# Attention followed by a gated squared-ReLU mixture on one core: one scale for each weight matrix, and two vector operands moved to PSUM

## The chip, the cores and the metric

The kernel runs on one core of a Trainium2 chip. The metric is the device time of one execution in microseconds (us); it ran three times before the change, and the profiled execution is a run of its own. The core has five engines that run their own instruction streams in order and wait for each other through semaphores: PE (TensorE, matrix products; PEld are its weight loads), DVE (VectorE), ACT (ScalarE), POOL (GpSimd) and SP (SyncE, which here only issues DMAs). PE writes PSUM, which has eight banks of 512 float32 columns here; DVE and ACT read and write both PSUM and SBUF.

## The reference, cut to what matters

The inputs are `q`, `k`, `v` of 8 batches x 12 heads x 448 tokens x 64, two gains, and the mixture's parameters. The three weight matrices arrive as 64-bit floats.

```python
def rmsnorm(x, g):
    rms = np.sqrt(np.mean(x * x, axis=-1, keepdims=True) + 1e-06)
    return x / rms * g
q_n, k_n = (rmsnorm(q, g_q), rmsnorm(k, g_k))
scores = scale * np.matmul(q_n, k_n.transpose(0, 1, 3, 2))
scores = scores - np.max(scores, axis=-1, keepdims=True)
attn = np.exp(scores)
attn = attn / (np.sum(attn, axis=-1, keepdims=True) + 1e-09)
x = np.matmul(attn, v)                  # then [8, 448, 768]: heads side by side
...
xk = mu_k * x + (1.0 - mu_k) * x_prev   # x_prev: the token before
xr = mu_r * x + (1.0 - mu_r) * x_prev
k = np.maximum(xk @ w_k, 0.0)           # 768 x 1024
v = k * k @ w_v                         # 1024 x 768
r = 1.0 / (1.0 + np.exp(-(xr @ w_r)))   # 768 x 768
return (r * v).astype(np.float32)
```

## The kernel before

**What a unit of work is.** The 96 heads are taken as 24 "quads" of two head pairs. `load` brings a quad's `q` and `k`, `stats` forms the sums of squares and their reciprocal roots (`rsqrt`: a first guess by integer arithmetic and three Newton steps, 13 small DVE instructions with two scalings ahead of them), `preps` scales `q` and `k` by them and turns them round, and `scores` makes seven groups of score tiles from each quad, two PSUM tiles of 448 columns a group: 168 groups, 336 score tiles. From the fourth quad on every float32 operand is split into two 16-bit parts (high and low) and a product is three 16-bit products. `expo` takes a score tile's maximum on DVE and its exponential on ACT, `probs` and `split` scale and split it, and `attends` multiplies a head pair's probabilities by `v` (48 of these; six make a batch).

**The mixture.** For each batch, `mixk` and `mixr` call `mix` six times each: one product with the earlier token on POOL, one multiply-add on DVE, the high part on ACT, the low part on POOL. That makes 96 mixes. `moe` then has two stages for a batch. The **first stage** multiplies by `w_k` (eight blocks of 18 matrix products, weights `wkh`/`wkl`) and squares the result (`square`). The **output stage** multiplies by `w_r` and `w_v` (weights `wrh`, `wrl`, `wvh`, `wvl`) and ends in `gate`, `store` and the output DMA. Because the first batch needs the weights, `moe` waits in the first batch for all of `w_k` before the first stage and for all 20 weight tiles (`st["wdone"] == NW`) before the output stage.

**The weights.** A tile is 128 columns of a matrix; `w_k` has 8 tiles, `w_r` and `w_v` 6 each. `wload` issues two DMAs a tile on ACT's queue, each of 3 or 4 runs of 1 KB a partition. `weights` turns each half tile from 64-bit to 32-bit floats: one byte's worth of low bits on POOL (written back into the raw buffer), the top word on ACT into a PSUM bank, and a shift-and-or of the two on DVE. `wsplit` then finds a power of two for the tile: the sums of squares of its columns as a matrix product with itself on PE, the diagonal on DVE (`dg`), a second product with ones to spread it over the partitions, a maximum and two small integer steps on DVE into `WSC`. With that scale it writes the high part (ACT) and the low part (DVE, or POOL together with the scaling, for tiles 1 to 13).

**What sets the order.** Nothing above runs in the order of the code. Each of these functions is a generator that yields its next instruction; the class `Plan` keeps an estimated clock for each engine and for each buffer, and takes again and again the instruction whose engine and operands are free earliest, less a priority. The priority of the weights (`wprio`) grows with the planned time and falls with each finished tile (`W_GAP`). The result is one fixed order for each engine, which the chip executes as it stands. The eight PSUM banks are one ring, from which "shares" take up to a number of banks: scores 5 (leaving one free), mixture 2, other 2.

Of the kernel before, what the change touches and what calls it, by code (L numbers as in the profile page):

```python
# [1 line left out]

# [29 lines left out]
WF_BUFS = 2  # L32
# [6 lines left out]
LOW_TILES = range(0, 20)  # L39
POOL_TILES = range(1, 14)  # L40
# [48 lines left out]
WB_A = 'ot'  # L89
WB_B = 'mm'  # L90
# [5 lines left out]
W_GAP = 10e3  # L96
# [108 lines left out]

class Plan:
    LAT = 35

    def __init__(self, tc):
        self.tc = tc  # L210
        self.clk = dict.fromkeys(("PE", "DVE", "ACT", "POOL", "SP"), 0.0)
        self.last, self.use, self.threads = {}, {}, []
        self.form, self.dma_free, self.acc, self.n = None, {"SP": 0.0, "ACT": 0.0}, False, 0
        self.held = {"DVE": [], "POOL": []}

# [13 lines left out]
    def spawn(self, gen, prio=0):  # L229
        th = [gen, prio, None, 0.0]  # L230
        self.threads.append(th)
        self.advance(th)
# [14 lines left out]
    def advance(self, th):  # L247
# [7 lines left out]
        th[2] = x  # L255
        th[3] = self.ready(x) if isinstance(x, list) else 0.0
# [68 lines left out]
    def run(self):  # L325
        while self.threads:
            best, key = None, None
            for th in list(self.threads):
# [11 lines left out]
                k = max(self.clk[th[2][0].eng] + wait, th[3] + slack) - PS * (th[1]() if callable(th[1]) else th[1])  # L340
# [100 lines left out]
def attn_moe_kernel(tc, q, k, v, g_q, g_k, mu_k, mu_r, w_k, w_v, w_r, out):  # L441
# [15 lines left out]
    banks = {n: Share(psum, *c) for n, c in (("sc", SC_SHARE), ("mm", MM_SHARE), ("ot", OT_SHARE))}  # L457
# [18 lines left out]
    for nm, kt, n in (("wk", ND, D_FF), ("wr", ND, D_MODEL), ("wv", NF, D_MODEL)):  # L476
        WS[nm] = (wpool.tile([P, kt, n], F16, name=nm + "h"), wpool.tile([P, kt, n], F16, name=nm + "l"))
# [9 lines left out]

    def WB(ci):
        return WB_A if ci < NF else WB_B

# [9 lines left out]
    def late():  # L500
# [21 lines left out]
        "raw": Ring(stage, [P, NF // 2, 2 * P], I32, "raw", RAW_BUFS, plan),  # L522
# [4 lines left out]
    for name, plan_ in (("kk", KK_LENT), ("xk", XK_LENT)):  # L527
# [5 lines left out]
        for n in plan_:  # L533
# [10 lines left out]
            if len(r.shape) == 3:  # L544
# [27 lines left out]
    def mu_stats():  # L572
        yield from until(lambda: st["lu"] >= 1 and len(WFT))
# [34 lines left out]
    def stats():  # L608
        for u in range(NQ):
# [4 lines left out]
            tm = small.tile([P, NSS], F32, name="stm", bufs=3)  # L614
# [11 lines left out]
            yield V.tensor_scalar(out=ss[:, 0:2 * NT], in0=ss[:, 0:2 * NT], scalar1=1.0 / HD, scalar2=1e-6, op0=ALU.mult, op1=ALU.add)  # L626
            yield V.tensor_scalar(out=ss[:, 2 * NT:NSS], in0=ss[:, 2 * NT:NSS], scalar1=gm[:, 3:4], scalar2=gm[:, 4:5], op0=ALU.mult, op1=ALU.add)
            yield from rsqrt(V, y, ss, tm, NEWTON_ON == "POOL" and G_)
# [322 lines left out]
    def mix(b, d, which, dst, df, cnt):  # L951
# [5 lines left out]
        yield G_.tensor_scalar(out=df, in0=xp, scalar1=sc[:, j + ND:j + ND + 1], scalar2=0.0, op0=ALU.mult, op1=ALU.add)  # L957
        yield V.scalar_tensor_tensor(out=df, in0=xc, scalar=sc[:, j:j + 1], in1=df, op0=ALU.mult, op1=ALU.add)
# [17 lines left out]
    def wload():  # L976
        for nm, w, kt, c, ci in WT:
            hk = kt // 2
            for i in range(0, kt, hk):
                yield from until(lambda: st["g"] >= W_G0 + W_G1 * ci and st["lu"] >= (LEAD_W if ci < W_L1 else LEAD_W + 1 if ci < W_L2 else LEAD_W + 2))  # L980
                raw = yield from R["raw"].get(ci < NF)
                yield A.dma_start(out=raw[:, 0:hk, :], in_=w[i * P:(i + hk) * P, c * P:(c + 1) * P].bitcast(I32).rearrange("(i p) n -> p i n", p=P))
                RAW[ci, i] = raw

    def weights():
        for nm, w, kt, c, ci in WT:
            f = yield from R["wf"].get(ci < NF)
            fi = f.bitcast(I32)
            hk = kt // 2
            for i in range(0, kt, hk):  # L990
                yield from until(lambda: (ci, i) in RAW and st["tq"] >= GATE_W)
                raw = RAW.pop((ci, i))
                r4 = raw[:, 0:hk, :].rearrange("p i (n two) -> p i n two", two=2)
                top, low = r4[:, :, :, 1], r4[:, :, :, 0]
                zb = yield from banks["mm"].get()
                z = zb[:, 0:hk * P].rearrange("p (i n) -> p i n", n=P)
                zi = z.bitcast(I32)
                if ci in LOW_TILES:
                    yield G_.tensor_scalar(out=low, in0=raw.bitcast(mybir.dt.uint8)[:, 0:hk, :].rearrange("p i (n b) -> p i n b", b=8)[:, :, :, 3], scalar1=-15.5, scalar2=2.0 ** -5, op0=ALU.add, op1=ALU.mult)
                    yield A.activation(out=z, in_=top.bitcast(F32), func=AF.Prelu, scale=F64_EXP, alpha=F64_NEG)  # L1000
                    yield V.scalar_tensor_tensor(out=fi[:, i:i + hk, :], in0=zi, scalar=3, in1=low, op0=ALU.logical_shift_left, op1=ALU.bitwise_or)
                else:
                    yield A.activation(out=z, in_=top.bitcast(F32), func=AF.Prelu, scale=F64_EXP, alpha=F64_NEG)
                    yield V.tensor_scalar(out=zi, in0=zi, scalar1=3, scalar2=None, op0=ALU.logical_shift_left)
                    yield V.scalar_tensor_tensor(out=fi[:, i:i + hk, :], in0=low, scalar=29, in1=zi, op0=ALU.logical_shift_right, op1=ALU.bitwise_or)
                R["raw"].put(raw)
                banks["mm"].put(zb)
            WFT[ci] = f
            plan.spawn(wsplit(nm, kt, c, ci, f), wprio)
# [4 lines left out]
    def wsplit(nm, kt, c, ci, f):  # L1014
        cs = slice(c * P, (c + 1) * P)
        wh, wl = WS[nm]
        f = f[:, 0:kt, :]
# [220 lines left out]
```

## Time and profile before

| | before |
|---|---|
| time, median of 3 runs (lowest, highest) | 1015.41 us (1015.3, 1017.15) |
| the profiled execution's own time | 1015.21 us |
| its span, first to last instruction | 1013.4 us |
| PE busy | 926.0 us, 91% |
| DVE busy | 812.7 us, 80% |
| ACT busy | 746.0 us, 74% |
| POOL busy | 691.8 us, 68% |
| mean clock granted to PE | 0.961 |

The times of the profile are positions in the span of one execution. Busy time is the time in which at least one instruction of an engine is under way, so instructions that overlap on an engine count once. All instructions of the planner carry one line of the source (the line that issues them), so the rows are told apart by their tiles: `ps` is any PSUM bank, `sums` the small maxima and sums of the scores, `nat` the buffers for probabilities and for `q` and `k` on their way, `stk` the finished `q` and `k`, `sst`, `stm` and `ss` the squares, the working tile and the result of the reciprocal root, `df` the buffer of a mix, `raw` and `wf` a weight tile before and after it is turned to 32 bits. A name that ends in x is a further buffer of the same kind.

### The profile page before, as it was taken

The numbers are of one execution on the slowest core, as the hardware profiler recorded it, in microseconds if no ns is written. First come the engines' busy times: TensorE is split into PE (matmuls) and PEld (weight loads), VectorE is DVE, ScalarE is ACT, GpSimd is POOL, SyncE is SP. The second block draws the span as 40 slices with busy tenths as digits, with TensorE's granted clock in tenths as the row PEclk, the third lists the DMA queues.
The fourth block names the chain that finished last, engine by engine and source line by source line (L and its number), as shares of the span: only waits on it lengthen the run. The fifth ranks groups of instructions, "written<-read, shape, count | busy, mean of one in ns | idle before, by whom it ended". The sixth has DMA issues, their size and how long they took to land. (4 is left out here: it accounts for less than half of the span.)

```text
span 1013.4 us, 18593 instructions
## 1 busy us (share of the span) xinstructions
PE 926.0 (91%) x6082; PEld 485.8 (48%) x6082; DVE 812.7 (80%) x2260; ACT 746.0 (74%) x1756; POOL 691.8 (68%) x734
## 2 busy tenths in 40 slices
PE   2588869669999999999999999899999999999998
PEld 2354434335544555455545555355545454455564
DVE  5879998999998698979997998799997989763000
ACT  3667878878788789888887887878886988952311
POOL 2787889743798747877886859855987478556501
PEclk9878979869999999999999999999999999999999
DMA  7322349667788789569847977869858884640000
GB/s 248 119 80 86 118 120 221 170 166 169 172 165 168 143 197 203 133 152 201 207 105 173 214 158 161 161 131 201 175 126 177 186 183 110 146 107 32 1 32 32
DMA packets 371138, 148.17 MB, mean 146 GB/s; under 512 B 338272, under 2 KB 355168, under 8 KB 371040
## 3 DMA queue, kind: packets, MB, share of 16 engines
q1 hardware_dynamic: 351792, 129.20, 57.0%
q10 hardware_dynamic: 19248, 17.77, 5.9%
q8 instruction: 48, 0.79, 0.3%
q14 instruction: 50, 0.41, 0.1%
HBM read 51.98 MB, written 11.01 MB: 62 GB/s over the span
## 5 line engine op out<-in xcount | busy, mean ns | idle before, releaser
L273 PE MATMUL ps<-wvh,kk 128*128 128x384 f16 x896 | 233.1, 326 | 0.8 <-DVE nat L273 0.8
L273 ACT ACTIVATE ps<-ps,sums 128x448 f32<-128x448 f32 x294 | 181.9, 621 | 52.5 <-DVE sums L273 48.9
L273 PE MATMUL ps<-xk,wkh 128*128 128x448 f16 x768 | 210.5, 356 | 4.8 <-DVE wf L273 3.9
L273 DVE SCALAR_TENSOR_TENSOR nat<-ps,sums,nat 128x64 f16<-128x64 f32 x480 | 190.7, 439 | 19.2 <-ACT nat L273 17.8
L273 DVE TENSOR_REDUCE sums<-ps 128x1 f32<-128x448 f32 x336 | 193.7, 612 | 15.4 <-PE ps L273 15.1
L273 PE MATMUL ps<-wrh,xr 128*128 128x384 f16 x672 | 179.9, 331 | 2.1 <-DVE nat L273 2.0
L273 ACT ACTIVATE nat<-ps,sums 128x448 f16<-128x448 f32 (+1 forms) x272 | 167.8, 659 | 16.9 <-DVE sums L273 7.1
L273 PEld LDWEIGHTS <-kk 128*128 128x128 f16 (+1 forms) x1362 | 129.2, 98 | 98.7 <-issue 13.5
L273 PE MATMUL ps<-stk 64*128 64x448 f16 (+3 forms) x1104 | 134.2, 390 | 26.4 <-ACT xk L273 6.2
L273 PE MATMUL ps<-wvl,kk 128*128 128x384 f16 x448 | 146.0, 326 | 0.0
L273 PE MATMUL ps<-xk,wkl 128*128 128x448 f16 x384 | 136.5, 355 | 0.0
L273 PEld LDWEIGHTS <-xr 128*128 128x128 f16 x1008 | 96.4, 99 | 80.1 <-issue 16.9
L273 PE MATMUL ps<-wrl,xr 128*128 128x384 f16 x336 | 111.1, 331 | 0.0
L273 PEld LDWEIGHTS <-wkh 128*128 128x128 f16 x768 | 71.9, 99 | 81.6 <-issue 21.6
L273 POOL TENSOR_TENSOR o<-o,bsc 128x384 f32<-128x384 f32 x48 | 43.3, 902 | 88.3 <-DVE o L273 52.3
L273 DVE SCALAR_TENSOR_TENSOR o<-o,ps 128x384 f32<-128x384 f32 x56 | 30.5, 545 | 87.7 <-PE ps L273 59.2
L273 PE MATMUL ps<-pT,vh 128*64 128x448 f16 x588 | 93.8, 363 | 1.4 <-DMA pT<-nat 0.7
L273 ACT ACTIVATE o<-ps,bsc 128x128 f32<-128x128 f32 x144 | 45.6, 387 | 51.2 <-PE ps L273 33.1
L273 POOL TENSOR_TENSOR qk<-qk,ss 128x896 f32<-128x896 f32 x36 | 64.0, 1778 | 22.1 <-DVE ss L273 14.9
L273 PEld LDWEIGHTS <-stk 64*128 64x128 f16 x1008 | 35.0, 98 | 78.0 <-issue 35.5
L273 DVE SCALAR_TENSOR_TENSOR df<-x,bsc,df 128x448 f32<-128x448 f32 x68 | 61.0, 910 | 5.8 <-POOL df L273 5.7
L273 POOL TENSOR_TENSOR nat<-nat 128x448 f32<-128x448 f32 x41 | 48.2, 1175 | 23.6 <-ACT nat L273 17.1
(161 smaller groups left out, 1813.7 us busy)
## 6 DMA issues: line engine op xcount, KB each, us to landing
vf<-in_v_dram SPq DMA_DIRECT2D x48, 256.0 KB, 3.0
out_dram<-o SPq DMA_DIRECT2D x28, 384.0 KB, 2.7
qk<-in_k_dram SPq DMA_DIRECT2D x23, 448.0 KB, 4.4
qk<-in_q_dram SPq DMA_DIRECT2D x22, 448.0 KB, 4.3
raw<-in_moe_w_v_dram ACTq DMA_DIRECT2D x12, 512.0 KB, 4.2
raw<-in_moe_w_r_dram ACTq DMA_DIRECT2D x12, 384.0 KB, 3.3
kk<-in_moe_w_k_dram ACTq DMA_DIRECT2D x8, 384.0 KB, 3.9
raw<-in_moe_w_k_dram ACTq DMA_DIRECT2D x8, 384.0 KB, 3.7
```

The source lines that it names most:

```text
L273: r = op.fn(op.kw["out"], op.kw["value"]) if op.fn.__name__ == "memset" else op.fn(**op.kw)
```

## The change

Five edits and a new plan:

1. **One scale for each matrix.** The sums of squares of all tiles of a matrix are added up in one PSUM bank (`pg`; four tiles side by side for `w_k`, one for the others), and `wscale` finds one power of two for the matrix: three times the chain of `dg`, product with ones, maximum and two integer steps, where there were twenty. A copy spreads the scale over the tiles' columns of `WSC`. `wsplit` can start only when the matrix's last tile is in, and takes the tiles of a matrix strictly one after the other (`st["wdone"] == ci`), because a tile in 32 bits now lies in the place where the next tile's two parts will lie. POOL splits the even tiles (ten instead of thirteen), ACT and DVE the odd ones.
2. **Weights laid out on the host.** The host puts each half tile's numbers of a partition side by side, so a DMA has one run a partition, and **SP** issues it, not ACT. POOL writes the low bits straight into the tile's place.
3. **The mix's first product** goes to ACT and into a PSUM bank (`df` share) instead of POOL and SBUF, and DVE's multiply-add reads it there.
4. **The reciprocal root of the squares of q and k** has its scaled input and its working tile in a PSUM bank (`df` share).
5. **Shares of the PSUM ring**: the 32-bit step of the weights gets its own (`wz`, 2), the sums of squares one (`pg`, 1, held from a matrix's first tile to its scale), and mixes and roots two (`df`, leaving one free).

The planner adds up to 10 ns drawn from a seeded random sequence to each instruction's key, and `W_GAP` falls from 10 to 7 us, so ties and near ties fall differently everywhere, and the whole order is a new one.

```diff
-WF_BUFS = 2
+WF_BUFS = 1
-LOW_TILES = range(0, 20)
-POOL_TILES = range(1, 14)
+WZ_SHARE = (2, 0)
+PG_SHARE = (1, 0)
+DF_SHARE = (2, 1)
+POOL_TILES = range(0, 20, 2)
-W_GAP = 10e3
+W_GAP = 7e3
+SEEDS = [232]
+AMP = 10.0
...
+        th[4] = self.noise()
-                k = max(self.clk[th[2][0].eng] + wait, th[3] + slack) - PS * (th[1]() if callable(th[1]) else th[1])
+                k = max(self.clk[th[2][0].eng] + wait, th[3] + slack) - PS * (th[1]() if callable(th[1]) else th[1]) + th[4]
...
-            tm = small.tile([P, NSS], F32, name="stm", bufs=3)
+            qs = yield from banks["df"].get()
+            sm, tm = qs[:, 0:NSS], qs[:, NSS:2 * NSS]
-            yield from rsqrt(V, y, ss, tm, NEWTON_ON == "POOL" and G_)
+            yield from rsqrt(V, y, sm, tm)
+            banks["df"].put(qs)
...
-        yield G_.tensor_scalar(out=df, in0=xp, scalar1=sc[:, j + ND:j + ND + 1], scalar2=0.0, op0=ALU.mult, op1=ALU.add)
-        yield V.scalar_tensor_tensor(out=df, in0=xc, scalar=sc[:, j:j + 1], in1=df, op0=ALU.mult, op1=ALU.add)
+        pb = yield from banks["df"].get()
+        yield A.activation(out=pb[:, 0:S], in_=xp, func=AF.Copy, scale=sc[:, j + ND:j + ND + 1])
+        yield V.scalar_tensor_tensor(out=df, in0=xc, scalar=sc[:, j:j + 1], in1=pb[:, 0:S], op0=ALU.mult, op1=ALU.add)
+        banks["df"].put(pb)
...
-                yield A.dma_start(out=raw[:, 0:hk, :], in_=w[i * P:(i + hk) * P, c * P:(c + 1) * P].bitcast(I32).rearrange("(i p) n -> p i n", p=P))
+                yield SP.dma_start(out=raw[:, 0:2 * hk * P], in_=w[c, h].bitcast(I32))
...
-            plan.spawn(wsplit(nm, kt, c, ci, f), wprio)
+            yield [T.matmul(form=("w", 110 * kt), out=pg[:, c % nb * P:(c % nb + 1) * P], lhsT=w16[:, i, :], rhs=w16[:, i, :], start=(c == 0 and i == 0), stop=(last and i == kt - 1)) for i in range(kt)]
+            if last:
+                plan.spawn(wscale(nm, kt, ci - c, ci + 1, pg, nb * P), wprio)
...
+    def wscale(nm, kt, c0, c1, pg, w):
+        sc = WSC[:, c0:c0 + 1]
+        sci = sc.bitcast(I32)
+        dg = small.tile([P, 4 * P], F32, name="dg", bufs=1)[:, 0:w]
+        yield V.tensor_tensor(out=dg.rearrange("p (b n) -> p b n", n=P), in0=pg[:, 0:w].rearrange("p (b n) -> p b n", n=P), in1=bcast(ident[:, :], w // P), op=ALU.mult)
+        yield T.matmul(form=("f", 200 + 1.7 * w), out=pg[:, 0:w], lhsT=ones.broadcast_to([P, P]), rhs=dg, start=True, stop=True)
+        yield V.tensor_reduce(out=sc, in_=pg[:, 0:w], axis=AX.X, op=ALU.max)
+        banks["pg"].put(pg)
+        yield V.tensor_scalar(out=sci, in0=sci, scalar1=24, scalar2=23, op0=ALU.logical_shift_right, op1=ALU.logical_shift_left)
+        yield V.tensor_scalar(out=sci, in0=sci, scalar1=-1.0, scalar2=float(204 << 23), op0=ALU.mult, op1=ALU.add)
+        yield V.tensor_copy(out=WSC[:, c0 + 1:c1], in_=sc.broadcast_to([P, c1 - c0 - 1]))
+        for ci in range(c0, c1):
+            plan.spawn(wsplit(nm, kt, ci - c0, ci, ci + 1 == c1), wprio)
+
+    def wsplit(nm, kt, c, ci, last):
+        yield from until(lambda: st["wdone"] == ci)
+        sc = WSC[:, ci:ci + 1]
+        f = WFT[nm].rearrange("p i n -> p (i n)")[:, 0:kt * P] if last else WS[nm][:, c + 1].rearrange("p a i n -> p (a i n)").bitcast(F32)
+        hi, lo = (WS[nm][:, c, a].rearrange("p i n -> p (i n)") for a in range(2))
```

How the order moves is seen at three places. The first is PE's stream where the first batch's output stage begins. Before, the rows are the last score group and the last tile's scale (`dg,ones`) and then the first product with `w_r` (weights `wrh`); ahead of it in the stream stand 76 score tiles (38 groups), 9 `attends` and all 20 products with ones:

```order
L273 MATMUL ps_2436<-stk_2259 128x448
L273 MATMUL ps_2413<-dg,ones 128x128
L273 LDWEIGHTS stk_2259
...
L273 MATMUL ps_2478<-stk_2259 128x448
L273 LDWEIGHTS stk_2259
L273 MATMUL ps_2477<-stk_2259 128x448
L273 LDWEIGHTS xr_1506
L273 MATMUL ps_2505<-wrh,xr_1506 128x384
```

In the change the same product follows directly on the score group that stands beside the eighth and last block of the first stage, with 64 score tiles (32 groups) and 7 `attends` ahead of it:

```order
L287 LDWEIGHTS stk_1385
L287 MATMUL ps_2117<-stk_1385 64x448
L287 LDWEIGHTS stk_1385
L287 MATMUL ps_2116<-stk_1385 64x448
L287 LDWEIGHTS xr_1648
L287 MATMUL ps_2139<-wr,xr_1648 128x384
```

Six score groups and two `attends` have moved from ahead of the output stage to behind its start. The first stage itself begins behind 50 score tiles before and 52 in the change, and ends with 64 in both.

The second place is DVE's stream while the first batch is mixed. Before, the Newton steps (`stm`, `ss`), the mixes (`df`) and a tile's scale (`WSC`) stand between the maxima of the scores:

```order
L273 TENSOR_TENSOR stm<-sst,ss 128x28
L273 RECIPROCAL sums_110<-sums_110 128x2
L273 SCALAR_TENSOR_TENSOR df_1425<-x_1209,bsc,df_1425 128x448
L273 SCALAR_TENSOR_TENSOR stm<-stm,ss 128x28
L273 TENSOR_REDUCE sums_105<-ps_1448 128x1
L273 SCALAR_TENSOR_TENSOR ss<-stm,ss 128x28
L273 SCALAR_TENSOR_TENSOR wf_1462<-ps_1463,raw_1381 128x384
```

In the change the mixes read a PSUM bank, and the tiles that are turned to 32 bits there are already those of `w_v`:

```order
L287 SCALAR_TENSOR_TENSOR df_1464<-x_838,bsc,ps_1468 128x448
L287 SCALAR_TENSOR_TENSOR wv<-ps_1479,wv 128x512
L287 TENSOR_REDUCE sums_107<-ps_1455 128x1
L287 TENSOR_SCALAR bstat<-bstat 128x1
L287 SCALAR_TENSOR_TENSOR nat_1403<-ps_1271,sums_105,nat_1403 128x64
```

So the 32-bit step of the weights runs ahead (12 tiles were through it at the start of the first stage before, all 20 are in the change), while the splitting comes later.

The third place is the start of SP's stream. Before, it holds only the loads of `q`, `k` and `v`:

```order
L273 DMA vf_95<-in_v_dram 128x512
L273 DMA qk_119<-in_k_dram 128x896
L273 DMA qk_159<-in_q_dram 128x896
L273 DMA qk_180<-in_k_dram 128x896
L273 DMA xk_104<-in_q_dram 128x896
```

In the change the weights' halves stand between them, and each waits in line for its raw buffer:

```order
L287 DMA raw_163<-in_moe_w_k_dram 128x768
L287 DMA qk_121<-in_q_dram 128x896
L287 DMA kk_100<-in_moe_w_k_dram 128x768 x2
L287 DMA raw_252<-in_moe_w_k_dram 128x768
L287 DMA raw_263<-in_moe_w_k_dram 128x768
L287 DMA qk_195<-in_k_dram 128x896
```

The 40 weight loads have left ACT's stream and now stand in SP's, ahead of some loads of `q` and `k`.

More of the change, by code (lines that the diff above doesn't have):

```diff
@@ L88 @@
 SLACK_F = 6
-WB_A = 'ot'
-WB_B = 'mm'
 LEAD_V = 1
@@ L521, in attn_moe_kernel @@
         "wf": Ring(stage, [P, NF, P], F32, "wf", WF_BUFS, plan),
-        "raw": Ring(stage, [P, NF // 2, 2 * P], I32, "raw", RAW_BUFS, plan),
+        "raw": Ring(stage, [P, NF * P], I32, "raw", RAW_BUFS, plan),
     }
@@ L985, in weights @@
     def weights():
         for nm, w, kt, c, ci in WT:
-            f = yield from R["wf"].get(ci < NF)
-            fi = f.bitcast(I32)
[L989 to L1005, printed above, removed]
@@ new lines, in weights @@
+            if c == 0:
+                pg = yield from banks["pg"].get()
+            last = ci + 1 in (NF, NF + ND, NW)
+            nb = 4 if ci < NF else 1
+            if last:
+                wf = yield from R["wf"].get(ci < NF)
+                f = wf.rearrange("p i n -> p (i n)")[:, 0:kt * P]
+                WFT[nm] = wf
+            else:
+                f = WS[nm][:, c + 1].rearrange("p a i n -> p (a i n)").bitcast(F32)
+            fi = f.bitcast(I32)
+            for h in range(2):
+                yield from until(lambda: (ci, h) in RAW and st["tq"] >= GATE_W)
+                raw = RAW.pop((ci, h))
+                n = kt * P // 2
+                cols = slice(h * n, (h + 1) * n)
+                zb = yield from banks["wz"].get()
+                z = zb[:, 0:n]
+                yield G_.tensor_scalar(out=fi[:, cols], in0=raw.bitcast(mybir.dt.uint8)[:, 0:8 * n].rearrange("p (n b) -> p n b", b=8)[:, :, 3], scalar1=-15.5, scalar2=2.0 ** -5, op0=ALU.add, op1=ALU.mult)
+                yield A.activation(out=z, in_=raw[:, 0:2 * n].rearrange("p (n two) -> p n two", two=2)[:, :, 1].bitcast(F32), func=AF.Prelu, scale=F64_EXP, alpha=F64_NEG)
+                yield V.scalar_tensor_tensor(out=fi[:, cols], in0=z.bitcast(I32), scalar=3, in1=fi[:, cols], op0=ALU.logical_shift_left, op1=ALU.bitwise_or)
+                banks["wz"].put(zb)
@@ L1011, in inverse @@
     def inverse(o, i):
         return V.tensor_scalar(out=o.bitcast(I32), in0=i.bitcast(I32), scalar1=-1.0, scalar2=float(0x7F000000), op0=ALU.mult, op1=ALU.add)
[L1014 to L1017, printed above, removed]
-        w16 = f.bitcast(BF16).rearrange("p i (n two) -> p i n two", two=2)[:, :, :, 1]
-        pg = yield from banks[WB(ci)].get()
-        yield [T.matmul(form=("w", 110 * kt), out=pg[:, 0:P], lhsT=w16[:, i, :], rhs=w16[:, i, :], start=(i == 0), stop=(i == kt - 1)) for i in range(kt)]
-        sc = WSC[:, ci:ci + 1]
-        sci = sc.bitcast(I32)
-        dg = small.tile([P, P], F32, name="dg", bufs=1)
-        yield V.tensor_tensor(out=dg, in0=pg[:, 0:P], in1=ident, op=ALU.mult)
-        yield T.matmul(form=("f", 400), out=pg[:, P:2 * P], lhsT=ones.broadcast_to([P, P]), rhs=dg, start=True, stop=True)
-        yield V.tensor_reduce(out=sc, in_=pg[:, P:2 * P], axis=AX.X, op=ALU.max)
-        banks[WB(ci)].put(pg)
+    def wscale(nm, kt, c0, c1, pg, w):
+        sc = WSC[:, c0:c0 + 1]
+        sci = sc.bitcast(I32)
+        dg = small.tile([P, 4 * P], F32, name="dg", bufs=1)[:, 0:w]
[3 more added lines that the diff above has]
+        banks["pg"].put(pg)
```

63 lines of the change are left out of this document (38 added, 25 removed).

## The prediction, made before the changed kernel ran

> **What bounds the kernel now.** I read the slices of the page first, then the busy times of longer stretches, then the rows of single tiles. The slices (25 us each) say which engine is full where:
>
> ```profile
> PE   2588869669999999999999999899999999999998
> DVE  5879998999998698979997998799997989763000
> PEclk9878979869999999999999999999999999999999
> ```
>
> From the tenth slice on PE stands at 9 almost without a break; before that it goes up and down while DVE is as full as later. The same in microseconds, by stretches cut where the work changes (columns: stretch, length, then busy time and count of PE, PEld, DVE, ACT, POOL, then PE's granted clock):
>
> ```profile
> 0.00:137.00 137.00, 93.45 (x531) 53.77 (x532) 113.70 (x327) 90.19 (x209) 95.61 (x126) 0.89 0.40 128
> 137.00:190.00 53.00, 43.53 (x271) 22.20 (x269) 46.31 (x119) 43.57 (x94) 49.91 (x51) 0.91 0.73 171
> 190.00:227.50 37.50, 23.03 (x133) 11.27 (x134) 34.35 (x101) 28.39 (x59) 19.54 (x22) 0.65 0.76 187
> 227.50:290.00 62.50, 61.84 (x428) 32.91 (x429) 60.41 (x177) 52.62 (x129) 38.28 (x38) 0.96 0.86 176
> 290.00:900.00 610.00, 595.49 (x4072) 303.07 (x4070) 541.46 (x1516) 505.20 (x1207) 444.49 (x452) 0.99 0.75 165
> 926.00:1013.40 87.40, 82.63 (x485) 47.24 (x483) 8.39 (x12) 18.14 (x43) 30.50 (x33) 1.00 0.06 23
> ```
>
> From 227.5 us on PE is the bound: 595.49 of 610 us busy. An engine that gets lighter there gives nothing. What can be won lies ahead of 227.5 us, and most plainly in 190 to 227.5, where PE is busy for 23.03 of 37.5 us at a clock of 0.65. Why it is empty there, the rows of the weights say (first the products with `wkh` in two stretches, then the span of the first products with `wrh` and of the last split of `w_v`, as first and last start):
>
> ```profile
> 180.00:190.00 10.00, 5.96 (x22) 1.97 (x21) 0.00 (x0) 0.00 (x0) 0.00 (x0) 1.00 0.29 88
> 190.00:200.00 10.00, 0.00 (x0) 0.00 (x0) 0.00 (x0) 0.00 (x0) 0.00 (x0) 0.66 1.01 239
> L273 PE MATMUL ps<-wrh,xr x672: 325/326/528, 227.5 to 1004.4; 128*128 128x384 f16 x168
> L273 DVE SCALAR_TENSOR_TENSOR wvl<-wf,WSC,wvh x6: 1276/1389/2156, 177.4 to 227.3; 128x1024 f16<-128x1024 f32 x6
> ```
>
> The first batch's first stage ends at 190 us, its output stage starts at 227.5, and the last of the 20 weight tiles is split at 227.3. For 37.5 us the mixture, which fills PE everywhere else, has nothing to run, and PE gets only what DVE (34.35 of 37.5 us busy) lets through of the scores.
>
> **The change, part by part.** The order shows the output stage right behind the first stage: 64 score tiles ahead of it, not 76, and the first stage at its old place (52 tiles ahead, not 50). So the question is whether all 20 weight tiles can be done by the time at which the first stage ends, and whether that time stays near 190 us. I count DVE's instructions up to the 64th score tile in both orders, since DVE was 46.31 of 53 and 34.35 of 37.5 us busy on either side of it. Rows for the prices:
>
> ```profile
> L273 DVE TENSOR_TENSOR dg<-ps,ident 128x128 f32<-128x128 f32 x20 | 5.6, 280 | 0.8 <-PE ps L273 0.8
> L273 DVE TENSOR_REDUCE WSC<-ps 128x1 f32<-128x128 f32 x20 | 5.7, 283 | 2.6 <-PE ps L273 2.5
> L273 DVE TENSOR_SCALAR WSC<-WSC 128x1 int32<-128x1 int32 x40 | 5.8, 144 | 0.2
> L273 DVE SCALAR_TENSOR_TENSOR ss<-stm,ss 128x28 f32<-128x28 f32 x72 | 22.3, 310 | 0.8
> L273 DVE TENSOR_SCALAR sums<-ps 128x2 f32<-128x2 f32 x147 | 21.9, 150 | 11.6 <-ACT ps L273 11.1
> L273 DVE TENSOR_SCALAR sums<-sums 128x2 f32<-128x2 f32 x21 | 8.9, 426 | 1.3 <-ACT nat L273 1.3
> L273 DVE SCALAR_TENSOR_TENSOR df<-x,bsc,df 128x448 f32<-128x448 f32 x68 | 61.0, 910 | 5.8 <-POOL df L273 5.7
> L273 DVE SCALAR_TENSOR_TENSOR o<-o,ps 128x384 f32<-128x384 f32 x56 | 30.5, 545 | 87.7 <-PE ps L273 59.2 <-issue 28.4
> L273 DVE SCALAR_TENSOR_TENSOR wvl<-wf,WSC,wvh 128x1024 f16<-128x1024 f32 x6 | 9.2, 1541 | 0.4 <-ACT wvh L273 0.4
> L273 DVE SCALAR_TENSOR_TENSOR wf<-ps,raw 128x384 int32<-128x384 int32 (+1 forms) x30 | 18.0, 600 | 0.7 <-issue 0.4 <-POOL raw L273 0.2
> ```
>
> - Scales: 16 tiles had been scaled by then, each with 280 + 283 + 2 x 144 = 851 ns, 13.6 us; three matrices take about 3.4 us (one of them with 512 columns). **-10.2 us.**
> - Reciprocal roots: 65 instructions before, at 280 to 500 ns, 20.2 us; 78 in the change, in PSUM. No row shows them there. The nearest is the same kind of small step on `sums`: 150 ns where it reads PSUM, 426 ns where it reads SBUF. Bounds 0.15 and 0.31 us (the `ss` row); I take 0.20, the PSUM row with 26 more columns and some slack: 15.6 us. **-4.6 us** (-8.5 to +4).
> - Mixes: 12 in both. 910 ns each before; with one operand in PSUM the `o` row has 545 ns for 384 columns, so 0.61 us for 448 (adding 64 columns at about 1 ns). **-3.5 us**, between nothing and that.
> - Splitting and the 32-bit step: 10 tiles split on DVE instead of 3 (seven of 768 columns at about 1.0, three at 1.54 us): +7.1 us. 40 halves turned instead of 33, at about 0.6 us: +4.8 us. **+11.9 us.**
> - The rest (copies of turned probabilities that fall to DVE instead of ACT, two more maxima of squares, the last scales of the batch): **+8.6 us.**
>
> The sum is +2.2 us: DVE does all the weights ahead of the mark for the price of four tiles less before. ACT gains 12 mix products at about 0.6 us (7.2 us) and the last tiles' parts, and loses its DMA issues: 38 before the mark, each
>
> ```profile
> L273 ACTq DMA_DIRECT2D raw<-in_moe_w_r_dram x12: 374/374/393, 80.6 to 144.9; - x12
> L273 POOL TENSOR_SCALAR df<-x,bsc 128x448 f32<-128x448 f32 x68 | 44.4, 661 | 5.3 <-DVE bsc L273 4.4
> L273 ACT ACTIVATE kf<-ps,RSC 128x448 f32<-128x448 f32 x46 | 29.8, 647 | 18.5 <-PE ps L273 11.7 <-POOL kk L273 6.5 <-issue 0.3
> L273 ACT CAST xk<-df 128x448 f16<-128x448 f32 x34 | 19.5, 594 | 9.8 <-DVE df L273 9.6
> ```
>
> at 0.374 us, 14.2 us that no busy time counts. POOL loses 12 products of 0.661 us and three split tiles, and is lighter by some 8 us. (The mix product on ACT is not in this trace; the casts at 594 ns and the scaled `kf` at 647 ns bound it, and I take 0.6.) So I let the first stage end where it ended, at 190 us, and **the gap of 37.5 us closes**.
>
> What stood in the gap does not vanish: six score groups, two `attends` and some transposes now run beside the output stage, on the engine that is the bound there. Their shares of PE's busy time:
>
> ```profile
> L273 PE MATMUL ps<-stk 64*128 64x448 f16 (+3 forms) x1104 | 134.2, 390 | 26.4 <-ACT xk L273 6.2 <-DMA stk<-natx 5.7 <-DVE natx L273 3.8
> L273 PE MATMUL ps<-pT,vh 128*64 128x448 f16 x588 | 93.8, 363 | 1.4 <-DMA pT<-nat 0.7 <-DVE o L273 0.7
> L273 PE MATMUL ps<-pT,vl 128*64 128x448 f16 x336 | 61.7, 363 | 0.0
> L273 PE MATMUL ps<-ident,nat 128*128 128x128 f32 x182 | 33.1, 327 | 25.4 <-DVE nat L273 19.5 <-POOL nat L273 4.8 <-ACT nat L273 0.7
> ```
>
> A score product takes 134.2 / 1104 = 0.122 us of it, six groups of six 4.4 us; an `attends` product 155.5 / 924 = 0.168 us, two of 22 products 7.4 us; four transposed PSUM tiles, some 14 products at 0.182 us, 2.5 us. Together 14.3 us, less if the slow clock of the early stretch has stretched these means (0.89 of full speed there: at worst a fourth less, 10.7). I take 12.5. The other weight products of the gap are done earlier, in time that PE has to spare. The 17 products with ones that go are no gain where PE waits for DVE.
>
> **The sum.** 1013.4 - 37.5 + 12.5 = 988.4 us of span. The profiled execution took 1015.21 us, 1.8 more than its span, and stands 0.2 below the median of the three runs, so the span's forecast becomes **990 us**.
>
> What I cost at nothing: the fewer runs a load has (loads land under decoding), the weight products that read three blocks of 128 columns instead of one of 384 (no row shows such a read; a slower one would show in every output stage), the mixes' lighter DVE work behind 227.5 us (PE covers it), and SP's longer queue. There a weight load waits for its raw buffer with loads of `q` and `k` behind it. These are wanted one quad later, and a quad's seven groups took over 30 us in this stretch (50 tiles in 141 us); if that cover were gone, one load's 4 us would stand open.
>
> [...]
>
> **The rivals.**
>
> *The gap closes only in part.* The split is now one chain: each tile waits for the one before, POOL, ACT and POOL in turn for the even ones, ACT and DVE for the odd ones, and `w_v` gets its scale only inside the first stage (its product with ones stands behind the first block). For it speaks that every hop joins a queue that is 80 to 95% full, and the first stage starts two score tiles later. Six tiles of `w_v` at 1.15 to 2.2 us a step are about 21 us of bare work, against 49 us of first stage (141 to 190). If the hops double that and the roots cost the upper bound, the output stage starts 10 to 20 us late: **1000 to 1010 us**.
>
> *It gains more.* Ahead of 190 us PE is idle for 53 us and DVE's mixes, roots and scales now hold it less; behind 227.5 us PE still has 15 us of idle time in 610. A third of both gives 20 us: **970 us**. Against it: DVE's sum ahead of the mark did not fall.
>
> *ACT becomes the bound: slower than before.* From the output stage's start to the end of the scores ACT gets 84 mix products more, 50.4 us, and the gap's own ACT work, at most 28.4 us. With the 557.8 us of the two stretches (52.62 + 505.20) that makes 636.6 us, in 672.5 + 14.3 = 687 us: 93%. The most that ACT shows in a hundred is this, DVE's most beside it:
>
> ```profile
> 200.00:300.00 100.00, 88.24 (x583) 45.78 (x582) 95.45 (x272) 80.20 (x186) 61.37 (x60) 0.88 0.79 175
> 400.00:500.00 100.00, 98.60 (x674) 50.91 (x672) 90.88 (x262) 85.89 (x205) 76.70 (x78) 1.00 0.76 166
> ```
>
> If 85.89% were all it can do, the stretch would take 741 us and the end come 54 us later, at **1044 us**. It decides from 636.6 / 710 = 90%: below that rate the whole gain is gone. Against it: DVE holds 95% over such a stretch, and ACT's busy time overstates what it must do when it is full. In the timeline (start, length)
>
> ```profile
> 227.12 0.60 ACT L273 ACTIVATE ps<-ps,sums 128x448 f32<-128x448 f32 x1
> 227.63 0.15 ACT L273 ACTIVATION_READ_ACCUMULATOR ps<-ps,sums 128x1 f32 x1
> 227.68 0.65 ACT L273 ACTIVATE nat<-ps,sums 128x448 f16<-128x448 f32 x1
> 228.20 0.63 ACT L273 ACTIVATE ps<-ps,sums 128x448 f32<-128x448 f32 x1
> ```
>
> an exponential, its accumulator and a split take 1.40 us by their lengths, but the next exponential starts 1.08 us after the first. At that pace 93% shrinks to some 75 to 85%.
>
> *It does not do what it says:* the gap closes, but the attention work drawn out of it delays the second batch's mix, and PE empties there instead: within 4 us of **1015 us**.
>
> **How the numbers follow.** Forecast (980 to 1000 us) 0.62, part of the gap 0.14, more gain 0.12, ACT the bound 0.08, no change 0.04. The bounds of the unknown prices (roots -8.5 to +4 us against the -4.6 taken, mixes up to 3.5 us dearer) move the output stage's start by -4 to +12 us, so 986 to 1002; two in ten are left out by a range of **973 to 1008 us**. About 0.2%, 2 us, can be told from no change here. Faster is the first three cases, most of each: 0.87; within it 0.05; slower 0.08.
>
> **What would show it.** In the profile after, `wr` with `xr` should first run within some 10 us of 190, right behind the last `wk` with `xk`, with the last split of `wv` some us ahead; PE's slices should stand at 9 from the eighth on with the clock at full; the `WSC` and `dg` rows should have 3 instances, the root rows about 200 ns and the mix rows about 610 ns; ACT should be busy for some 90% from there to the end of the scores, and PE idle no more than 2 to 3% in that stretch. An output stage that starts at 205 us or later, or PE rows waiting for ACT in the dense stretch, would make the prediction wrong.

## The result and the profile after

The changed kernel is slower, where the forecast was 990 us and faster: **1027.72 us** in the median of four runs (1027.48 to 1027.89) against 1015.76 (1015.3 to 1017.15), a ratio of 1.0115, 95% interval 1.0098 to 1.0133. The profiled span grew from 1013.4 to 1025.7 us. Every run in this document had a mean granted clock of 0.95 to 0.98 but one, the second run of the first experiment, which took 1209.79 us at 0.749 and is compared with none. First the slices of the page of the changed kernel (25.6 us each):

```profile
PE   0787759899898999999899998989999999999998
DVE  4898888788886898898978988799947887712000
ACT  2678799888997998999898988999886888824311
PEclk9898969999999999999999999999999999999999
```

The hole that PE had before 227.5 us is gone, but from the ninth slice on PE falls to 8 again and again, where the kernel before stood at 9. The stretches say the same in microseconds, cut at the first stage's start, at the output stage's start, and at 290 us (columns as before: stretch, length, busy time and count of PE, PEld, DVE, ACT, POOL, then PE's clock, the DMA share and GB/s):

```profile
0.00:158.00 158.00, 97.97 (x585) 54.33 (x586) 128.44 (x351) 110.59 (x249) 104.09 (x138) 0.88 0.56 170
158.00:198.00 40.00, 37.30 (x226) 18.28 (x227) 31.80 (x84) 37.35 (x76) 35.76 (x30) 0.96 0.44 91
198.00:290.00 92.00, 85.91 (x582) 44.69 (x582) 79.38 (x231) 80.09 (x189) 53.86 (x56) 0.98 0.77 154
290.00:890.00 600.00, 565.38 (x3881) 284.87 (x3880) 501.38 (x1509) 526.99 (x1249) 365.87 (x361) 0.99 0.84 166
```

Where the two stages begin is in the rows of the weights (first and last start):

```profile
L287 PE MATMUL ps<-xk,wk x1152: 349/352/581, 158.0 to 965.6; 128*128 128x448 f16 x192
L287 PE MATMUL ps<-wr,xr x1008: 322/326/527, 198.0 to 1016.4; 128*128 128x384 f16 x168
L287 DVE SCALAR_TENSOR_TENSOR wv<-wf,WSC,wv x1: 1956/1956/1956, 193.6 to 193.6; 128x1024 f16<-128x1024 f32 x1
```

The output stage starts at 198.0 us, right behind the first stage and the last split: the gap did close. The whole run is then three numbers, the start of the output stage, PE's busy time from there to its last product, and PE's idle time in the same stretch, for which these are the rows, first of the kernel before, then of the changed kernel:

```profile
227.50:1008.60 781.10, 765.94 (x5149) 398.56 (x5149) 617.74 (x1715) 583.84 (x1398) 525.96 (x537) 0.99 0.66 146
```

```profile
198.00:1020.60 822.60, 781.01 (x5238) 404.68 (x5237) 597.82 (x1769) 645.07 (x1525) 463.55 (x465) 0.99 0.71 142
```

| | start of output stage | busy from there | idle from there | tail | span |
|---|---|---|---|---|---|
| before | 227.5 | 765.9 | 15.2 | 4.8 | 1013.4 |
| forecast | 190.0 | 778.4 | 15.2 | 4.8 | 988.4 |
| after | 198.0 | 781.0 | 41.6 | 5.1 | 1025.7 |

Of the 37.3 us between forecast and result 8.0 are the later start, 2.6 the attention work that was drawn out of the gap, and **26.4 us are new idle time of PE in the dense stretch**. What ends it there (PE's waits in 290 to 890 us; columns: total us, times, longest), before:

```profile
PE ps L273 <- DMA stk<-natx: 5.7, 2, 3.8
PE ps L273 <- DVE natx L273: 3.8, 4, 1.8
PE ps L273 <- DVE nat L273: 2.9, 5, 0.8
```

and after:

```profile
PE ps L287 <- DVE nat L287: 15.5, 22, 2.3
PE ps L287 <- ACT o L287: 3.0, 2, 2.3
PE ps L287 <- DVE vs L287: 2.4, 2, 1.3
PE ps L287 <- ACT kf L287: 2.2, 1, 2.2
```

For 15.5 of its 34.6 us of idle time in this stretch PE waits for DVE's split of the probabilities (`nat`), behind which a bank comes free, though DVE got lighter (501.38 us of 600, 531.55 before). The rest is spread over many small waits, 8.7 us of them for ACT. DVE in turn waits more than before. Its rows in the same stretch that matter here, before

```profile
DVE nat L273 <- ACT nat L273: 16.8, 24, 1.9
DVE sst L273 <- POOL nat L273: 12.8, 7, 3.1
DVE sums L273 <- ACT ps L273: 8.7, 14, 1.2
```

and after:

```profile
DVE sums L287 <- ACT ps L287: 23.3, 39, 2.2
DVE sst L287 <- POOL nat L287: 23.1, 9, 9.6
DVE nat L287 <- ACT nat L287: 18.7, 31, 2.6
```

`sums<-ps` is the step that takes the two sums of a score group from the exponentials; it stood waiting for an unfinished exponential 14 times before and 39 times after. Three causes were possible: ACT with the mix products is late (A), the banks held by mixes and roots are missing (D), or the new order is a worse one (C, L). The letters in the expectations below are not the same throughout: in the first two experiments (one move undone, the random term) B is the order and C the banks; where each part is planned alone, C is the order and B the cost of the one scale.

### The profile page after: what moved, and what is told of

It reads as the page before. It is cut to its first block, busy times and chain, and to the rows that moved or that the text cites. A ratio compares the mean times of both kernels' runs of the same rounds, so it can differ in the third digit from the quotient of the medians.

```text
span 1025.7 us, 18552 instructions
## 1 busy us (share of the span) xinstructions
PE 916.3 (89%) x6048; PEld 477.3 (47%) x6048; DVE 758.6 (74%) x2203; ACT 793.0 (77%) x1847; POOL 604.2 (59%) x632
## 5 line engine op out<-in xcount | busy, mean ns | idle before, releaser
L287 PE MATMUL ps<-xk,wk 128*128 128x448 f16 x1152 | 230.8, 356 | 11.5 <-DVE vs L287 5.0
L287 PE MATMUL ps<-wv,kk 128*128 128x384 f16 x1344 | 233.8, 326 | 3.9 <-DVE nat L287 2.7
L287 DVE SCALAR_TENSOR_TENSOR nat<-ps,sums,nat 128x64 f16<-128x64 f32 x492 | 194.8, 442 | 27.5 <-ACT nat L287 26.6
L287 ACT ACTIVATE nat<-ps,sums 128x448 f16<-128x448 f32 (+1 forms) x280 | 171.9, 656 | 19.6 <-DVE sums L287 11.6
L287 PE MATMUL ps<-wr,xr 128*128 128x384 f16 x1008 | 180.6, 330 | 6.6 <-DVE nat L287 2.2
L287 PEld LDWEIGHTS <-wk 128*128 128x128 f16 (+1 forms) x1194 | 112.9, 99 | 127.7 <-issue 25.3
L287 POOL TENSOR_TENSOR o<-o,bsc 128x384 f32<-128x384 f32 x48 | 39.8, 830 | 133.8 <-DVE o L287 99.0
L287 PEld LDWEIGHTS <-stk 64*128 64x128 f16 x1008 | 34.5, 97 | 82.4 <-issue 39.9
L287 PE MATMUL ps<-ident,nat 128*128 128x128 f32 x196 | 35.4, 323 | 32.4 <-DVE nat L287 12.3
L287 ACT ACTIVATE ps<-x,bsc 128x448 f32<-128x448 f32 x96 | 61.8, 659 | 2.4 <-DVE nat L287 0.9
L287 PE MATMUL ps<-pT,vl 128*64 128x448 f16 x336 | 60.6, 352 | 0.0
L287 POOL TENSOR_TENSOR kf<-kf 128x448 f32<-128x448 f32 x46 | 43.5, 946 | 28.6 <-ACT kk L287 27.4
```

The lines of the kernel that those rows point to most:

```text
L287: r = op.fn(op.kw["out"], op.kw["value"]) if op.fn.__name__ == "memset" else op.fn(**op.kw)
```

## The experiments

**Undoing one operand move in the changed kernel's order.** Every engine keeps the order of the changed kernel and only the one instruction goes elsewhere; the planner still counts the price and the bank of the original.

```diff
-yield A.activation(out=pb[:, 0:S], in_=xp, func=AF.Copy, scale=...)
+yield G_.tensor_scalar(out=df, in0=xp, scalar1=..., scalar2=0.0, op0=ALU.mult, op1=ALU.add)
```

> The order of every engine is the changed kernel's; only the 96 first products of the mixes are issued on POOL into SBUF instead of ACT into PSUM (their place in the order kept, the PSUM bank still held). Theory A, the 62 us of mix products make ACT too full, and PE waits for what ACT does for the mixture (gates, squares) and the scores: PE's idle time between 290 and 890 us falls from 34.6 to 15-20 us and the time to 1003-1013 us. Theory B, the new order itself is the worse one, whoever computes the product: the time stays within 5 us of 1027.7. Theory C, the PSUM banks that mixes hold are missed by the scores: as B, since the banks are still held.

Measured: 1075.29 us, 48 above the changed kernel; all three theories missed. The multiply-add of the mix took 1116 ns here (910 before, 674 in the changed kernel):

```profile
L293 DVE SCALAR_TENSOR_TENSOR df<-x,bsc,df 128x448 f32<-128x448 f32 x68 | 75.7, 1116 | 18.4 <-POOL df L293 16.8 <-POOL x L293 1.4
L293 POOL TENSOR_SCALAR df<-x,bsc 128x448 f32<-128x448 f32 x68 | 49.7, 734 | 3.4 <-DVE bsc L293 1.6 <-ACT x L293 0.3
```

The second one puts the roots' operands back to SBUF, in the same way:

> The order of every engine is the changed kernel's; only the reciprocal roots work in SBUF again (310 small DVE instructions). Theory A (ACT) and B (order): DVE has room, the root rows go from about 190 to 280 ns, some 30 us more of DVE's time in 750, and the time moves by 0 to +6 us. A rival, that DVE's access to PSUM slows what it stands beside: the time falls by 5 us or more.

Measured: 1051.11 us, 23 above the changed kernel, ratio to the kernel before 1.0350 (1.0298 to 1.0402); the 0 to +6 us of both theories and the rival's fall are missed. A root's step, which has 193 ns in PSUM, has 287 here:

```profile
L293 DVE TENSOR_TENSOR stm<-sst,ss 128x28 f32<-128x28 f32 x72 | 20.7, 287 | 1.4
```

So in a fixed order the two moves help, the mix product by 48 us and the roots by 23. What is worth 23 us in one order, though, is worth nothing in the orders below that were planned for it (1021.09 us without the roots in PSUM, 1021.77 with them, everything else alike): an edit undone in the order of another kernel does not price the edit.

**The random term.** The seed set to 0 (no term), and to 7:

```diff
-SEEDS = [232]
+SEEDS = [0]
```

> The changed kernel planned without the random term in the keys, so another order of the same work. Theory A (ACT too full): within 6 us of 1027.7, since the load is the same. Theory B (this order is a bad draw): 1000-1015 us.

> The changed kernel with another seed (7 for 232). Theory A: within 6 us of 1027.7. Theory B: it differs by 8 us or more from 1027.7 or from the kernel without the random term; the spread of these three orders says what an order alone is worth.

Measured: 1021.77 us without the term (ratio 1.0067, 1.0041 to 1.0093), 1036.95 with the other seed (1.0211, 1.0135 to 1.0287). Without the term A's range is just met and B's is missed; with the other seed A is missed and B met. The same edits move by 15 us with the order alone, more than the 12 us between the two kernels.

**Each part alone, planned anew, without the random term.** Edits 1, 2 and 5 (with the changed kernel's other settings, `W_GAP` of 7 us among them); these with the roots; these with the mix product; and edits 3 and 4 on the kernel before.

> Edits 1, 2 and 5 alone (one scale for each matrix, weights through SP, the shares of the ring), planned anew without the random term; the mix's first product stays on POOL and in SBUF, the roots stay in SBUF. To be read beside the same plan with all edits (1021.8 us, output stage from 201.0, PE idle 21.2 us in 290-890). Theory A, the mix product makes ACT too full and PE waits for it: here ACT is as light as before, so the gap at 190-227 us closes and the dense stretch costs nothing: 990 to 1005 us, PE idle in 290-890 at most 18 us. Theory B, the one scale and its serial split delay the start and the operand moves only help: slower than with all edits, 1025 to 1045 us, first stage at 158 us or later. Theory C, the order alone: within 1010 to 1037 us with no pattern.

> As the kernel with one scale alone, and the roots of q and k in PSUM as well (mix product on POOL and in SBUF); planned anew without the random term. Theory A (ACT too full): the best of the four, 985 to 1003 us. Theory B (the one scale costs, the operand moves help): 5 to 20 us below the one with the scale alone, above the 1021.8 of all edits. Theory C: no pattern.

> As the kernel with one scale alone, and the mix's first product on ACT and in PSUM as well (roots in SBUF, 280 to 310 ns a step); planned anew without the random term. Theory A: 10 us or more above the one with the scale alone, ACT 525 us or more busy in 290-890. Theory B: 5 to 20 us below the one with the scale alone. If the 23 us that the roots cost in SBUF at the kept order are a price of the operand, this one is about 20 us above all edits (1042); if they were a price of an order laid out for cheap roots, it is within 8 us of 1022.

> Edits 3 and 4 alone on the kernel before: mix product on ACT and in PSUM, roots in PSUM; 20 scales, weights through ACT's queue, old shares (and one of two banks for mixes and roots), planned anew. The gap ahead of the output stage stays. Theory A (ACT too full): 1025 us or more, PE idle in 290-890 at least 25 us. Theory B (the one scale costs, the operand moves help): 990 to 1010 us, first stage at 141 us or earlier. Theory C: 1005 to 1030.

Measured: 1008.40 us for one scale alone (ratio 0.9919, 0.9875 to 0.9962), **faster than both kernels**; 1024.14 (1.0086) with the roots, 1021.09 (1.0059) with the mix product, and 1015.97 (1.0005) for the operand moves without the one scale. A's range is met with the mix product alone (ACT 533.1 us busy in 290-890) and missed in the other three, B's is missed in all four; only C, the order's luck, fits them roughly (1008.40 lies just below its range). With the mix product alone the roots stand in SBUF, and the time is within 1 us of all edits without the term, not 20 above; that was expected if the 23 us were the price of an order laid out for cheap roots. The row of one scale alone from its output stage's start:

```profile
198.90:1001.80 802.90, 779.55 (x5245) 405.92 (x5244) 654.49 (x1786) 603.24 (x1445) 544.87 (x554) 0.99 0.67 147
```

It starts its output stage as late as the changed kernel and has as much work left, but only 23.3 us of idle time in place of 41.6.

**ACT's load or the bank.** The mix product on ACT without a bank, and a bank held without the product on ACT:

```diff
-yield G_.tensor_scalar(out=df, in0=xp, ...)
+yield A.activation(out=df, in_=xp, func=AF.Copy, scale=...)
```

```diff
+pb = yield from banks["df"].get()
 yield G_.tensor_scalar(out=df, in0=xp, ...)
 yield V.scalar_tensor_tensor(out=df, in0=xc, scalar=..., in1=df, ...)
+banks["df"].put(pb)
```

> As the kernel with one scale alone (1008.4 us), but the mix's first product on ACT and into SBUF: ACT gets the 96 products, no bank is taken for them; planned anew, no random term. Theory A (ACT's load empties PE): as with the product in PSUM, 1018 to 1028 us, PE idle behind the output stage's start 32 us or more (23.3 with one scale alone, 35.2 with the product on ACT and in PSUM). Theory D (the bank that mixes and roots hold is missing to the scores, PE waits for banks): 1004 to 1012 us, idle 20 to 26 us. Theory C (the order alone): anywhere from 1005 to 1037 us.

> As the kernel with one scale alone, product on POOL and in SBUF, but each mix holds one PSUM bank from before its product to behind its multiply-add without using it: the bank is taken, ACT is as light as before; planned anew, no random term. Theory A (ACT's load): 1004 to 1012 us. Theory D (banks): 1018 to 1028 us, PE idle behind the output stage's start 30 us or more. Theory C: anywhere from 1005 to 1037 us.

Measured: 1019.68 us (1.0037) and 1019.27 (1.0042), the same time by different ways. The first is what A said and D did not, the second is D's time and not A's, with a little less idle time than D's 30 us. The rows from the output stage's start, ACT's load first, then the bank:

```profile
191.60:1012.80 821.20, 782.23 (x5257) 405.87 (x5256) 646.86 (x1806) 652.98 (x1545) 492.24 (x471) 0.99 0.66 144
```

```profile
200.80:1013.00 812.20, 783.63 (x5249) 407.30 (x5245) 652.60 (x1785) 607.12 (x1445) 540.99 (x553) 0.98 0.68 145
```

With the product on ACT PE is idle for 39.0 us, with the bank alone for 28.6, against 23.3 with neither. The idle time points to ACT's load more than to the bank, in one order each; the times don't tell them apart, since the first starts its output stage 9 us earlier.

**Three orders for each combination.** One scale alone with both seeds, then the kernel before and the operand moves alone with both:

> The kernel with one scale alone, planned with the random term of the seed that gave 1037 us with all edits (and 1021.8 without the term). If the 13 us between one scale alone (1008.4) and all edits (1021.8) are the operands' price, this one is 10 to 25 us below 1037, at 1012 to 1027; if they are the order's luck, it is as likely above 1021 as below.

> The kernel with one scale alone, planned with the random term of the changed kernel (1027.7 us with all edits). If the operand moves cost 10 us or more whatever the order: 1005 to 1018 us; if the difference is luck of the order: anywhere from 1005 to 1037.

> The kernel before, planned with the changed kernel's random term (seed 7). Theory L (the order before was a good draw, and any new plan loses some 10 us): 1020 to 1040 us, PE idle behind the output stage's start 25 us or more. Theory E (the edits themselves cost): 1010 to 1020 us, idle 12 to 20 us, as without the term (1015.7, 15).

> As the one before, with the seed of the changed kernel (232). Theory L: 1020 to 1040 us, idle 25 us or more. Theory E: 1010 to 1020 us, idle 12 to 20 us.

> Edits 3 and 4 alone (mix product on ACT and in PSUM, roots in PSUM) on the kernel before, seed 7. If the operand moves add some 10 us of idle time to PE behind the output stage's start whatever the rest (as they did with one scale, 11 us in the mean of three orders, and 6 without the random term here): idle 5 to 17 us above the kernel before with the same seed, and the time 0 to 12 us above it. If they do not: within 4 us of its idle.

> As the one before, with seed 232: idle 5 to 17 us above the kernel before with the same seed if the operand moves cost, within 4 us if not.

Measured, time in us and, behind the stroke, PE's idle time from the output stage's start:

| | no random term | seed 7 | seed 232 |
|---|---|---|---|
| before | 1015.7 / 15.2 | 1031.9 / 25.9 | 1044.1 / 34.2 |
| operand moves (3, 4) | 1016.0 / 21.2 | 1056.0 / 38.5 | 1043.3 / 37.5 |
| one scale (1, 2, 5) | 1008.4 / 23.3 | 1028.5 / 28.4 | 1030.9 / 35.4 |
| all edits | 1021.8 / 34.5 | 1037.0 / 44.5 | **1027.7 / 41.6** |

The idle time is that of the profiled run. Where a time has two runs they lie within 2.9 us of each other, but for 5 us in all edits with seed 7 and 10 us in the operand moves with seed 232 (1038.34, which was profiled, and 1048.27).

The kernel before with the changed kernel's own seed is the slowest of its row, 1044.12 us (1.0286, 1.0230 to 1.0342), with the edits left out. Its row:

```profile
234.90:1039.00 804.10, 769.86 (x5129) 398.70 (x5127) 621.14 (x1703) 584.61 (x1392) 527.39 (x535) 0.99 0.64 141
```

Theory L's figures are met or passed by both orders of the kernel before, and one scale alone with the changed kernel's seed is slower than the changed kernel, which no price of the operand moves explains. The operand moves' own forecast came out half: with seed 7 the idle time rose by 12.6 us as forecast, but the time by 24 where 0 to 12 were forecast; with seed 232 the idle time rose by 3.3 us, which was to mean that they cost nothing. Three effects can be read off the table, each as a mean of differences within a column or a row:

- The random term adds 22 us (5.9 to 40.0, all eight differences above zero) and 12 us of idle time.
- The operand moves add 7 us (-3.2 to +24.1, six differences) and 9 us of idle time (3.3 to 16.1, all six above zero).
- The one scale takes 9 us off (-19.0 to +5.8, six differences). From its parts: the output stage starts 25.6 us earlier (16.8 to 32.0), PE has 10.9 us more work left from there, and 5.9 us more idle time.

The single differences scatter by some 10 us about their means. The random term's price is clear of that scatter, while the operand moves' price in time is not, and that of the one scale hardly is.

**What the random term does.** Its largest draw is 10 ns, but where two candidates of the planner stand equal, any draw decides, and without it the older one goes first. One kernel with a draw of at most 0.001 ns, and one with 10 ns that is the same for all pieces of one function (drawn anew after every 50 instructions), both on the kernel before with seed 232:

```diff
-AMP = 10.0
+AMP = 0.001
```

```diff
-... + th[4]
+... + self.noise(th[0].__name__)
```

> The kernel before, seed 232, with a random term of at most 0.001 ns in place of 10: it can only decide between candidates whose keys are equal. Of the 5663 choices that the planner makes for the kernel before, 972 are such ties, and the oldest piece of work wins them; with this term a younger piece of the same function goes ahead of an older one 458 times (455 with 10 ns). Theory T (ties among peers cost): 1027 to 1050 us, PE idle behind the output stage's start 25 us or more, about as with 10 ns (1044). Theory U (any disturbance costs, in proportion): 1012 to 1025.

> The kernel before, seed 232, with a random term of 10 ns that is the same for all pieces of one function and drawn anew after every 50 instructions: the order between different kinds of work is disturbed as much as before (nearly half of PE's rows and most of the other engines' stand elsewhere), but no younger piece goes ahead of an equal older one of its own function. Theory T: 1010 to 1025 us, idle 12 to 22 us. Theory U: 1027 us or more, idle 25 us or more.

Measured: 1030.53 us (1.0147, 1.0078 to 1.0216) with the ties alone, 1025.96 (1.0102, 1.0027 to 1.0176) with everything but the ties among equals. The first lies in theory T's range, with 26.4 us of idle time; the second lies between the two ranges, with 21.6 us, which is inside T's. In these single orders the ties cost 15 us of the 28, and disturbing everything else 10. The ties leave a mark. In DVE's order the changed kernel takes the younger of two score groups first (`sums_105` is the group behind `sums_104`):

```
TENSOR_REDUCE sums_105<-ps_3024
TENSOR_REDUCE sums_104<-ps_3003
...
TENSOR_SCALAR sums_105<-ps_3024
TENSOR_SCALAR sums_104<-ps_3003
...
SCALAR_TENSOR_TENSOR nat_3112<-ps_3024,sums_105,nat_3112
SCALAR_TENSOR_TENSOR nat_3111<-ps_3004,sums_104,nat_3111
```

Counted over the whole order, 77 of 588 splits stand behind a split of a younger group. In the eight orders with the term of 10 ns it is 77 to 107 and in the ties-only order 100; with the term that keeps equals in order it is 4, and in the orders without a term none. DVE's waits for an unfinished exponential in 290 to 890 us (first column us, second their number) rise with it, from 14 before to 39 in the changed kernel. With all edits but no random term:

```profile
DVE sums L287 <- ACT ps L287: 11.5, 22, 1.4
```

with the kernel before and seed 7, where ACT has none of the mix products:

```profile
DVE sums L287 <- ACT ps L287: 20.6, 38, 2.2
```

with one scale alone and no random term:

```profile
DVE sums L287 <- ACT ps L287: 5.9, 12, 1.0
```

with the ties alone:

```profile
DVE sums L287 <- ACT ps L287: 23.1, 36, 2.5
```

and with everything but the ties:

```profile
DVE sums L286 <- ACT ps L286: 12.5, 18, 1.8
```

So the late exponentials that the changed kernel's profile shows are mostly the sign of the order, not of ACT's load: the operand moves alone, with ACT as full (530.75 us busy in 290 to 890 us, 526.99 in the changed kernel), have 27 such waits, and with the mix product and one scale it is 19. Their number doesn't give PE's idle time, though: the mix product on ACT and in SBUF has 15 of them and 39.0 us of idle time, the kernel before with seed 7 has 38 and 25.9. By which waits a worse order empties PE was not isolated.

## Why the prediction was wrong

The time went outside the range of 973 to 1008 us. From the kernel before to the changed one there are three steps, each a run: 1015.7 to 1008.4 us (one scale), to 1021.8 (operand moves), to 1027.7 (random term). The steps are not the parts' prices: by another way through the table, the random term first, they are 28 us up, 13 down for the one scale and 3 down for the operand moves.

- **The step that failed** is the sum, "1013.4 - 37.5 + 12.5": under "From 227.5 us on PE is the bound" it carried PE's 15.2 us of idle time over unchanged, and put no price on the whole order being a new one, though the change said that it is. In its place the runs showed 23.3 us with one scale, 34.5 with the operand moves and 41.6 with the random term. The term on PE's idle time should have had a range of its own: over the twelve orders it is 15 to 45 us, and the kernel before is the lowest of them. The changed kernel's time lies in the middle of the three orders of its edits; the kernel before is the best of its three by 16 us. The prediction's own mark, PE idle for no more than 2 to 3% of the dense stretch, failed with 5.1% (41.6 of 822.6 us). Its sign of being wrong, PE rows that wait for ACT there, showed only in part: in 290 to 890 us PE waited 8.7 us for ACT (1.1 before) and 23.7 us for DVE (6.9 before).
- **The start of the output stage was mis-sized by 8 us**, in the step "so I let the first stage end where it ended". The sum beneath it was right: DVE was busy for 160.0 us before 190 us, and for 128.44 + 31.80 = 160.2 before 198 us, where +2.2 had been forecast (+1.6 if its seven further halves are taken at the 0.6 us that it names). But equal work is not an equal date: DVE had 7.8 us more idle time, and the first stage began at 158.0 us, not 141. Of the forecast gain of 37.5 us at this place six pairs of orders give 25.6 in the mean. No edit is needed for such a delay: the random term alone puts the first stage of the kernel before at 154.3 us (seed 7) and at 157.2 (seed 232), and 141 is the earliest of all orders run:

```profile
L287 PE MATMUL ps<-xk,wkh x768: 349/352/581, 157.2 to 983.8; 128*128 128x448 f16 x192
```

What delays it in each order was not isolated; in the changed kernel ACT was busy for 147.9 of the 198 us, where it had 133.8 of 190, and the loads on SP's queue were not put back on ACT's.
- **The moved attention work was right**: 12.5 us forecast, 15 in the changed kernel, 10.9 in the mean of the six pairs.
- **The prices were right**, within 11%: the mix product took 659 ns on ACT (0.6 us forecast), the multiply-add 674 (0.61 us), the root steps 184 to 193 (0.20 us), and the weights in three blocks of 128 cost nothing (322/326/527 ns, 325/326/528 before):

```profile
L287 ACT ACTIVATE ps<-x,bsc 128x448 f32<-128x448 f32 x96 | 61.8, 659 | 2.4 <-DVE nat L287 0.9 <-DVE ss L287 0.7 <-DVE bsc L287 0.6
L287 DVE SCALAR_TENSOR_TENSOR df<-x,bsc,ps 128x448 f32<-128x448 f32 x68 | 45.4, 674 | 13.2 <-ACT ps L287 10.9 <-POOL xk L287 1.2 <-POOL xr L287 0.2
L287 DVE TENSOR_TENSOR ps<-ps,ss 128x28 f32<-128x28 f32 x72 | 13.9, 193 | 1.4
```

- **The rival "ACT becomes the bound"** had the right sign with a wrong mechanism. It made 85.89% the most that ACT can do; the changed kernel shows 91.78% in the same hundred, with PE at 95.40%:

```profile
400.00:500.00 100.00, 95.40 (x659) 47.08 (x658) 87.48 (x264) 91.78 (x217) 66.58 (x63) 1.00 0.87 177
```

Both operand moves, ACT's load among them, add 9 us of idle time to PE in the mean, not 54.

What stays open: how much of the random term's price is ties (15 us) and how much any other disturbance (10 us), since each was one order; by which waits a new order empties PE; whether the operand moves cost time at all, and if so, whether ACT's load or the banks make them, where only the idle time speaks, for ACT.

## What to carry to other kernels

Where a planner lays out the order, an edit brings a new order with it, and its luck (here 15 to 40 us between the best and the worst of three orders of the same edits) can be larger than the edit: compare several orders of each version before pricing a part, and give the range of the dense stretch's idle time a term of its own. Here the fullest engine had more to lose from a reordering than to win from lighter neighbours: in the kernel before PE was busy for 98% from the output stage's start (765.94 of 781.10 us), had 15 us of idle time to win there and stood idle for up to 45 us in the other orders, and in the changed kernel a DVE lighter by 30 us in 600 (501.38 against 531.55) came with more of PE's idle time, not less. Among candidates of equal rank let the oldest go first: a random draw among them of at most 0.001 ns put 100 of 588 splits behind a younger group's and cost 15 us in the one order tried.

## What was not expected of the hardware

One instruction, the multiply-add of a mix with both operands in SBUF, took 910 ns in the kernel before, 1116 in the changed kernel's order with the product on POOL, and 674 with one operand in PSUM; the float32 steps of a root took 270 to 293 ns in SBUF and 184 to 193 in PSUM, in the same order. With both operands in SBUF the multiply-add still took 938 ns where the product came from ACT instead of POOL (DVE as a whole was busy for 646.86 us from the output stage's start, 654.49 with the product on POOL). What the instructions wait for in SBUF no run here separates.
